# ELU of the second products on ScalarE and VectorE alone, with difference steps and buffers moved

## The chip, the cores and the metric

The kernel runs on one core of a Trainium2 chip. The metric is the time of one execution on the device, in microseconds (us), as the median of several runs. The engines are TensorE (PE; its weight loads stand apart as PEld), VectorE (DVE), ScalarE (ACT), GpSimd (POOL) and the queue of SyncE (SP), which here only issues transfers.

## What is computed

The reference is attention in which a query sees only the keys of its own cluster, and behind it a two-layer network with ELU between the layers. All is float32; the network has 3072 tokens, a width of 512 and a hidden width of 2048.

```python
scores = np.where(mask, scale * np.matmul(q, k.transpose(0, 1, 3, 2)), -1000000000.0)
attn = softmax(scores)                      # rows; mask: same cluster
x = np.matmul(attn, v)                      # (4, 8, 768, 64) -> (3072, 512)
h = x @ w_in                                # (3072, 2048)
g = np.where(h > 0.0, h, np.exp(np.minimum(h, 0.0)) - 1.0)
out = g @ w_out                             # (3072, 512)
```

## The kernel before

**Stages.** First come 32 attention blocks. Then the network follows in three pairs of 512-token groups, numbered k_ = 0 to 5. For each pair a first product computes h for 1024 tokens at once, and two second products (one for each k_) multiply ELU(h) by w_out. Both kinds of product are one level of a fast matrix product with seven multiplications in place of eight, and the second products use it on two levels.

**First products.** The one for k_ = 0 and 1 (`first_pair`) is plain float32. Those for k_ = 2, 3 and 4, 5 (`k_phase(0)` and `k_phase(1)`) multiply in a packed form: each operand of tokens is split into three parts (`x_split`, four steps: ScalarE, VectorE, ScalarE, VectorE) in a buffer `xh0` or `xh1` of 3 x 1024 columns, in turn, and the split weights are read from memory into a ring of three slots (`w_ring`, two loads for a unit, 512 KB and 256 KB). A phase has 28 units; seven operands serve four units each. `minus` steps on VectorE make the token differences. TensorE writes into four double banks; ScalarE scales one bank into another (L1378), VectorE adds results (L1341). The result is four quadrants of h: c11, c21 (used by the even k_) and c12, c22 (used by the odd k_), 8 x 512 columns each.

**ELU.** For c11 and c21 of the packed products, ELU is in the phase itself: `k_exp` (ScalarE Exp, then a POOL TENSOR_SCALAR that cuts at 1) and `k_elu` (one VectorE end, L1150). For c12 and c22 it comes later, in parts of 128 x 1024 elements:

- of the first pair, c22 in `second_product_first` through `elu_steps` (`k_exp` and `k_elu`, four parts), while c12 is done in `first_pair` with two ScalarE steps (Exp, and Relu of 1 - e, L1269 and L1270) and one VectorE end (`first_elu`, L1411);
- of the later pairs in the even second product through `elu_in_products`: three parts of c12 by Exp and Relu on ScalarE, a POOL TENSOR_SCALAR (L1488) and a DMA that POOL issues and that adds into the target (L1491); the other five parts by `k_exp` and `k_elu`.

**Second products.** `second_product_first` runs the first three units (M1, M2, M3) of k_ = 0 directly. Then `chain` runs units back to back, seven a k_ in the order M1, M2, M3, M7, M6, M5, M4. A unit has seven small products m1 to m7 of 128 x 128 tiles. m1 and m5 of the next unit are issued inside the present one, so the order on TensorE is m6, m2, next m1, m7, next m5, m3, m4. VectorE makes four differences for the next unit (`t_step`, L1588 t1, L1590 t2, L1592 t3, L1594 t4, 128 x 512), adds what ScalarE set aside (L1544, L1561), and adds results (`take`, L1620; sums L1639); ScalarE copies banks (L1500, L1504, L1537, L1558). m5 needs the next unit's t1, m6 its t2, m7 its t3, m4 its t4, and each t overwrites what the present unit's product has just read. Behind m6, m2, m7 and m4 of each unit, `note` places other work by a table: the block differences `g_step` (L1606, two halves of 128 x 1024 each), the late ELU and, in k_ = 3, splits for the next packed product. The order on each engine is the order in which the program issues.

`table_first` and `table_last` make weight sums for the second level (L930 to L937 on VectorE; L997 and accumulating DMAs L999 issued by POOL) and `weigh_step` the sums L402 to L406. Weight tables are kept in memory and read back (L1079).

**Buffers.** When the first two second products are over, the pool that holds `p_out` (4608 columns; the output rows of k_ = 0 and 1 lie in the first 2048, t of k_ = 1 behind them) and `spare` (3072 columns) is released, and a new pool takes its bytes from the low end up. A tile of the new pool waits for users of old tiles on its bytes:

```python
k_e[:] = [lowest.tile([P, 2, 512], F32, name=f"k_e{n}") for n in range(2)]
xh.append(lowest.tile([P, 3, 2, 512], F32R, name="xh1"))
w_ring.append(lowest.tile([P, 3, 512], F32R, name="ring2"))
aside_of[1] = lowest.tile([P, 1024], F32, name="aside")
k_load(2, (0, 1), nc.scalar)
k_load(2, (2,), nc.scalar)
```

So `k_e` lies on the output rows, `xh1` on the rest of p_out and 512 columns of spare, `ring2` and `aside` on spare. The two loads into `ring2` are issued by ScalarE ahead of its work for the packed product.

## Time and profile before

| | us |
|---|---|
| median of 3 runs | 880.17 (877.0 to 880.77) |
| the profiled execution | 877.92 |
| its span in the trace | 876.2 |
| TensorE busy | 844.6 |
| VectorE busy | 762.9 |
| ScalarE busy | 495.0 |
| POOL busy | 171.6 |

Times in rows are us from the span's start; a group's row ends with busy time and the mean of one instruction in ns, and the engine's idle time just before such instructions, with what ended it. In the trace k_ = 0's direct units begin at 421.2, the first packed product at 520.3, the pair k_ = 2, 3 of second products at 603.4, the second packed product at 699.6 and the pair k_ = 4, 5 at 777.2. Names in rows are those of the tiles at the program's level: xT, kq_g and w_in hold other things by then (kq_g holds c11 and c21, w_in holds c12 and c22, and xT tokens, outputs, t and streamed weights).

### The profile page before, as it was taken

The page shows a single profiled execution, that of the slowest core. Times are in us where ns is not written, and L with a number is a line of the kernel's source. Part 1 is how long each engine was busy: PE and PEld are TensorE (multiplying, and loading weights), DVE is VectorE, ACT ScalarE, POOL GpSimd, SP SyncE. Part 2 cuts the span into 40 slices and gives each one's busy share as a digit, 9 for nine tenths or more (in the row PEclk, how much of TensorE's full clock was granted, in tenths as well). Part 3 has the DMA queues.
Part 4 walks back from the last instruction along what each step waited for, and adds up shares of the span by engine and source line. Part 5 has one row for each costly group of instructions (what it writes and reads, how often), then busy time and mean ns, then how long its engine had stood idle before and what let it go on. Part 6 is the DMA issues. An engine that isn't in the chain of part 4 may idle for free.

```text
span 876.2 us, 15157 instructions
## 1 busy us (share of the span) xinstructions
PE 844.6 (96%) x5584; PEld 590.2 (67%) x5584; DVE 762.9 (87%) x987; ACT 495.0 (57%) x813; POOL 171.6 (20%) x165
## 2 busy tenths in 40 slices
PE   9999999999999999999989998999989999998897
PEld 5444444444444443444889987878989988788897
DVE  6899999999998968978988876989998869899976
ACT  6887878786888864625431226665423266655121
POOL 0023230421223532110320000104420000044200
PEclk9999999999999999999999999999999999999999
DMA  7786796788679993999199967999967799849673
GB/s 170 158 208 177 165 254 173 158 203 189 161 217 285 303 261 128 274 281 279 42 190 252 291 205 241 290 286 326 271 182 230 215 286 296 278 118 282 166 242 129
DMA packets 185441, 194.06 MB, mean 221 GB/s; under 512 B 97680, under 2 KB 131472, under 8 KB 184336
## 3 DMA queue, kind: packets, MB, share of 16 engines
q1 hardware_dynamic: 174688, 163.32, 62.1%
q0 software_dynamic: 9552, 28.32, 16.2%
q10 hardware_dynamic: 1120, 1.38, 0.6%
q8 instruction: 46, 0.75, 0.4%
q14 instruction: 35, 0.29, 0.1%
HBM read 130.06 MB, written 51.38 MB: 207 GB/s over the span
## 4 chain that ended last, share of the span: by engine, by line
PE 71%; DVE 18%; DMA 4%; issue 3%; ACT 2%; POOL 1%; DVEq 0%; SPq 0%; POOLq 0%; ACTq 0%
PE bank L1099 20%; PE double L1331 15%; PE banks L540 11%; PE banks L1280 8%; PE o_bank L596 8%; PE d_bank L596 3%; PE banks L553 3%; DVE kq_g L1606 2%; DVE xT L1588 2%; DVE xT L1594 1%; DVE xT L1592 1%; PE d_bank L616 1%; PE banks L454 1%; DVE sums_w L580 1%; DMA k_s<-spare 1%
## 5 line engine op out<-in xcount | busy, mean ns | idle before, releaser
L1331 PE MATMUL double<-xh,ring 128*128 128x512 f32 x672 | 156.1, 393 | 4.9 <-ACT kq_g L1378 3.6
L1331 PEld LDWEIGHTS double<-xh,ring 128*128 128x128 f32 x672 | 126.7, 189 | 33.6 <-ACT kq_g L1378 4.0
L576 ACT ACTIVATE p_out<-banks 128x768 f32<-128x768 f32 x150 | 118.8, 813 | 10.0 <-PE banks L540 7.5
L596 PE MATMUL o_bank<-p_out,kq_g 128*64 128x384 f32 x600 | 102.3, 490 | 0.0
L1147 POOL TENSOR_SCALAR k_e<-k_e 128x1024 f32<-128x1024 f32 x26 | 32.6, 1258 | 274.1 <-ACT k_e L1146 274.1
L1099 PE MATMUL bank<-xT 128*128 128x128 f32 x640 | 81.6, 276 | 3.5 <-DVE xT L1588 2.8
L596 PEld LDWEIGHTS o_bank<-p_out,kq_g 128*64 128x64 f32 x600 | 40.8, 137 | 59.0 <-issue 55.7
L1099 PEld LDWEIGHTS bank<-xT 128*128 128x128 f32 x640 | 76.3, 192 | 4.2 <-DVE xT L1588 3.2
L1378 ACT ACTIVATE double<-double 128x1024 f32<-128x1024 f32 x52 | 52.3, 1009 | 43.1 <-PE double L1331 27.3
L1280 PE MATMUL banks<-xT,w_in 128*128 128x512 f32 x128 | 56.2, 595 | 2.0 <-DVE kq_g L1257 1.4
L1341 DVE TENSOR_TENSOR kq_g<-double,kq_g 128x1024 f32<-128x1024 f32 x36 | 44.0, 1221 | 11.8 <-PE double L1331 7.0
L580 DVE TENSOR_TENSOR sums_w<-p_out 128x1536 f32<-128x1536 f32 x25 | 46.2, 1848 | 9.2 <-ACT p_out L576 9.2
L1099 PE MATMUL bank<-w_out,xT 128*128 128x128 f32 x288 | 38.6, 277 | 9.2 <-DVE xT L1588 9.0
L1537 ACT COPY bank<-bank 128x128 f32<-128x128 f32 x39 | 9.8, 250 | 65.6 <-PE bank L1099 65.6
L1280 PEld LDWEIGHTS banks<-xT,w_in 128*128 128x128 f32 x128 | 24.0, 190 | 33.6 <-issue 28.8
L583 DVE TENSOR_TENSOR sums_w<-sums_w,p_out 128x1536 f32<-128x1536 f32 x25 | 44.3, 1772 | 1.8
L659 POOL DMA_DIRECT2D sums_b<-xT x28 | 17.9, 661 | 139.3 <-DVE xT L633 92.3
L654 POOL TENSOR_TENSOR xT<-xT,sums_b 128x384 f32<-128x384 f32 x32 | 43.6, 1380 | 5.0 <-DMA sums_b<-xT 3.4
L1099 PEld LDWEIGHTS bank<-w_out,xT 128*128 128x128 f32 x288 | 35.0, 192 | 10.3 <-DVE xT L1588 7.4
L540 PE MATMUL banks<-x_sum,xT 64*128 64x384 f32 x192 | 38.2, 486 | 0.7 <-ACT p_out L576 0.7
L540 PE MATMUL banks<-kq_g,xT 64*128 64x384 f32 x192 | 37.6, 483 | 0.0
L540 PE MATMUL banks<-x_sum,kq_g 64*128 64x384 f32 x192 | 37.5, 482 | 0.0
(321 smaller groups left out, 1815.6 us busy)
## 6 DMA issues: line engine op xcount, KB each, us to landing
ring<-k_s SPq DMA_DIRECT2D x32, 512.0 KB, 4.7
xT<-far_s_s SPq DMA_DIRECT2D x63, 256.0 KB, 3.6
kq_g<-in_v_dram SPq DMA_DIRECT2D x32, 384.0 KB, 5.0
ring<-k_a SPq DMA_DIRECT2D x23, 512.0 KB, 5.0
xT<-far_s_q SPq DMA_DIRECT2D x38, 256.0 KB, 3.4
xT<-far_a_s SPq DMA_DIRECT2D x37, 256.0 KB, 3.6
ring<-k_s SPq DMA_DIRECT2D x32, 256.0 KB, 4.4
k_a<-w_in SPq DMA_DIRECT2D x24, 256.0 KB, 7.1
```

Of the source, the lines that this page charges most:

```text
L540: nc.tensor.matmul(s[:, e, :HS], lhsT=kT[b % 2][pr][rows, ts(kt, P)], rhs=qT[half][pr][rows], start=first, stop=not first,)
L576: nc.scalar.activation(probs(n, kt), s[:, :, :HS], Act.Exp, scale=SCALE)
L580: nc.vector.tensor_tensor(add_four, p[0], p[1], op=Alu.add)
L583: nc.vector.tensor_tensor(add_four, add_four, four(n)[2], op=Alu.add)
L596: nc.tensor.matmul(value_bank(n)[64 * e : 64 * e + 64, :HS], lhsT=v_raw[n % 2][:, e, kt], rhs=probs(n, kt)[:, e], start=(kt == 0), stop=(k ...
L654: nc.gpsimd.tensor_tensor(x_of(n), x_of(n), r, op=Alu.mult)
L1099: nc.tensor.matmul(bank[:, :P], lhsT=left[:, f], rhs=right[:, f], start=first and f == 0, stop=last and f == 3, skip_group_check=True,)
L1147: nc.gpsimd.tensor_scalar(k_e[u % 2], k_e[u % 2], 1.0, 0.0, op0=Alu.min, op1=Alu.max)
L1280: nc.tensor.matmul(bank[:, j], lhsT=w[a][:, ch, QS * u + P * j : QS * u + P * j + P], rhs=x[:, ch], start=ch == 0, stop=ch == 1,)
L1331: nc.tensor.matmul(bank[:, j], lhsT=w[:, m, QS * ch + P * j : QS * ch + P * j + P], rhs=x[:, m, ch], start=first and ch == 0 and m == part ...
L1341: nc.vector.tensor_tensor(to, x, y, op=Alu.add)
L1378: nc.scalar.activation(at(into[0], u) if n < 2 else b, a, Act.Copy, scale=K_OF)
```

## The change

- Every late ELU part takes three steps: ScalarE Exp, ScalarE Relu (scale -1, bias 1), one VectorE end (`first_elu`). `elu_steps`, `elu_in_products`, their POOL steps and accumulating DMAs go. c12 is done in four parts of two blocks as before, c22 in four parts by columns (its left half, used by b21, first).
- Their places: c22's left half of the first pair in `second_product_first` and at m4 of unit 3 of k_ = 0, its right half in unit 0 of k_ = 1; for the later pairs parts 0 to 5 (and the ScalarE steps of part 6) in the even product, the end of part 6 and part 7 in unit 0 of the odd product.
- `g_step`: the first differences of k_ = 0 move from behind unit 0 to unit 2; in the other products the eight halves run from m7 of unit 0 to m2 of unit 4, one or two a unit, instead of two in each of units 1 to 4.
- In the packed products the split of the second operand has its steps at n = 0, 2, 3, 4 instead of 0, 0, 1, 1, and `minus` of the first phase at n = 0, 1, 3, 6 instead of 0, 1, 2, 3.
- The split buffers are three tiles each. In the lower pool the order is now ring2, aside (512 columns instead of 1024), xh1, k_e: ring2 lies on the output rows, k_e on spare, and xh1 where it was.

```diff
-            plan(on_act, 4 * i, x_split, q, 0)
-            plan(on_dve, 4 * i, x_split, q, 1)
-            plan(on_act, 4 * i + 1, x_split, q, 2)
-            plan(on_dve, SECOND_PART[i], x_split, q, 3)
-        for n, x in enumerate(((t1, x12, x11), (t2, x22, t1), (x12, x22, x12), (x21, x21, t2))):
+            for what, (of, n) in enumerate(zip((on_act, on_dve, on_act, on_dve), SPLIT_AT[i])):
+                plan(of, n, x_split, q, what)
+        for n, x in zip(
+            ((0, 1, 3, 6), (0, 1, 2, 3))[part],
+            ((t1, x12, x11), (t2, x22, t1), (x12, x22, x12), (x21, x21, t2)),
+        ):
             plan(on_dve, n, minus, *x)
...
-    SECOND_PART = (1, 5, 10, 14, 17, 22)
+    SPLIT_AT = [(0, 2, 3, 4)]
+    SPLIT_AT += [(4 * n, 4 * n, 4 * n + 1, m) for n, m in ((1, 5), (2, 10), (3, 14), (4, 17), (5, 22))]
...
+    def relu_of_exp(step, x, e):
+        if step == 0:
+            nc.scalar.activation(e, x, Act.Exp)
+        elif step == 1:
+            nc.scalar.activation(e, e, Act.Relu, scale=-1.0, bias=ones[:, :1])
+        else:
+            first_elu(x, e)
+
+    def late_part(n):
+        if n < 4:
+            return of_unit(s_of[2], n)
+        n -= 4
+        return s_of[3][:, 4 * (n % 2) : 4 * (n % 2) + 4, QS * (n // 2) : QS * (n // 2) + QS]
...
-            if at in ("m2", "m7") and n == 1:
-                g_step(k_, 3, at == "m7")
-            elif at in ("m2", "m7") and 2 <= n <= 4:
-                g_step(k_, (0, 2, 1)[n - 2], at == "m7")
-            if k_ >= FIRST_IN and not k_ % 2:
-                elu_in_products(n, at)
+            for step, x in ELU_STEPS[1 if k_ == 1 else 2 + k_ % 2].get((n, at), ()):
+                late_elu(step, x, dead_e[x % 2] if k_ == 1 else k_e[x % 2])
+            if (n, at) in G_STEPS:
+                g_step(k_, *G_STEPS[n, at])
...
+    for x, n, to in (
+        (0, 0, (0, "m4")),
+        (1, 1, (2, "m4")),
+        (2, 2, (3, "m4")),
+        (3, 3, (5, "m6")),
+        (4, 4, (5, "m4")),
+        (5, 5, (6, "m7")),
+    ):
+        for step, at in enumerate(((n, "m6" if n < 5 else "m2"), (n, "m2" if n < 5 else "m7"), to)):
+            even.setdefault(at, []).append((step, x))
+    for step, at in enumerate(((6, "m6"), (6, "m2"))):
+        even.setdefault(at, []).append((step, 6))
+    odd[0, "m6"] = [(2, 6), (0, 7)]
+    odd[0, "m2"] = [(1, 7)]
+    odd[0, "m4"] = [(2, 7)]
...
+    AT_FIRST = {(0, 1): [(0, 4)], (0, 2): [(1, 4)], (1, 0): [(0, 5)], (1, 1): [(1, 5)], (2, 3): [(2, 4)]}
...
-                if n > 0 or q_ in (1, 3):
-                    next(rest_of_elu, None)
+                for x in AT_FIRST.get((n, q_), ()):
+                    late_elu(*x, k_e[x[1] % 2])
+                if n == 2 and q_ in (1, 2):
+                    g_step(0, 0, q_ - 1)
...
-                for part in range(2):
-                    g_step(0, n, part)
...
+    w_ring.append(lowest.tile([P, 3, 512], F32R, name="ring2"))
+    aside_of[1] = lowest.tile([P, 512], F32, name="aside")
+    xh.append([lowest.tile([P, 2, 512], F32R, name=f"xh1{x}") for x in "hlm"])
     k_e[:] = [lowest.tile([P, 2, 512], F32, name=f"k_e{n}") for n in range(2)]
-    xh.append(lowest.tile([P, 3, 2, 512], F32R, name="xh1"))
-    w_ring.append(lowest.tile([P, 3, 512], F32R, name="ring2"))
-    aside_of[1] = lowest.tile([P, 1024], F32, name="aside")
```

More of the change, by code (lines that the diff above doesn't have):

```diff
@@ L1132, in x_split @@
         src, to = k_operands(part)[i], xh[q % 2]
[L1133 removed]
+        h, l = (x.bitcast(F32) for x in to[:2])
         if n == 0:
[L1135 removed]
+            split_minus(to[0], src)
         elif n == 1:
[L1137 removed]
+            nc.vector.tensor_tensor(to[1], src, h, op=Alu.add)
         elif n == 2:
[L1139 removed]
+            nc.scalar.activation(to[1], l, Act.Copy, scale=-4096.0)
         else:
[L1141 to L1143 removed]
+            nc.vector.scalar_tensor_tensor(to[2], h, -1.0, l, op0=Alu.mult, op1=Alu.subtract)
     def k_exp(x, u):
@@ L1160, in ahead_of_k @@
             )
-            xh.append(upmost.tile([P, 3, 2, 512], F32R, name="xh0"))
+            xh.append([upmost.tile([P, 2, 512], F32R, name=f"xh0{x}") for x in "hlm"])
             w_ring.extend(upmost.tile([P, 3, 512], F32R, name=f"ring{x}") for x in range(2))
@@ L1257, in result @@
                 nc.vector.tensor_tensor(to, bank, of_unit(plus[i], u), op=Alu.add)
-            if i == 5:
-                late_elu.append(of_unit(c22, u))
             if i in (1, 5, 6):
@@ L1298, in first_pair, with in_columns, late_elu @@
         assert not wait
-    late_elu = []
-    def elu_steps():
-        for n in range(len(late_elu) + 2):
-            if n > 1:
-                k_elu(late_elu[n - 2], n)
-            if n < len(late_elu):
-                k_exp(late_elu[n], n)
-            yield
+    def relu_of_exp(step, x, e):
[5 more added lines that the diff above has]
+            first_elu(x, e)
+    def in_columns(x):
+        if x.shape[1] == 2:
+            return x.rearrange("p a (b n) -> p a b n", b=2)
+        return x.rearrange("p (a b) n -> p a b n", a=2)
+    def late_part(n):
[3 more added lines that the diff above has]
+        return s_of[3][:, 4 * (n % 2) : 4 * (n % 2) + 4, QS * (n // 2) : QS * (n // 2) + QS]
+    def late_elu(step, n, e):
+        x = late_part(n)
+        if n > 3:
+            x, e = in_columns(x), in_columns(e)
+        relu_of_exp(step, x, e)
     def k_phase(part):
@@ L1449, in note @@
                     table_last("a22", last, 1)
+                    late_elu(2, 5, k_e[1])
                 elif (n, at) == (5, "m6"):
@@ L1480, in main_path @@
     }
-    def elu_in_products(n, at):
-        c12, c22 = s_of[2:]
-        if n in (0, 2, 4) and at in ("m6", "m2"):
-            x, e = of_unit(c12, n // 2), k_e[0]
-            if at == "m6":
-                nc.scalar.activation(e, x, Act.Exp)
-                nc.gpsimd.tensor_scalar(e, e, 1.0, -1.0, op0=Alu.min, op1=Alu.add)
-            else:
-                nc.scalar.activation(x, x, Act.Relu)
-                nc.gpsimd.dma_start(x, e, accum_op=Alu.add)
-        of = [*(of_unit(c22, u) for u in range(4)), of_unit(c12, 3)]
-        if at == "m6" and 0 < n < 6:
-            k_elu(of[n - 1], 1)
-        elif at == "m7" and n < 5:
-            k_exp(of[n], 1)
+    G_STEPS = {
+        (0, "m7"): (3, 0),
+        (1, "m2"): (3, 1),
+        (1, "m7"): (0, 0),
+        (2, "m2"): (0, 1),
+        (2, "m7"): (1, 0),
+        (3, "m2"): (2, 0),
+        (3, "m7"): (2, 1),
+        (4, "m2"): (1, 1),
+    }
+    dead_e = [X[:, 2 * n : 2 * n + 2, :GS] for n in range(2)]
+    even, odd = {}, {}
+    for x, n, to in (
[13 more added lines that the diff above has]
+    odd[0, "m4"] = [(2, 7)]
+    after_first = {
+        (0, "m6"): [(0, 6)],
+        (0, "m2"): [(1, 6), (0, 7)],
+        (0, "m7"): [(1, 7), (2, 6)],
+        (0, "m4"): [(2, 7)],
+    }
+    ELU_STEPS = [{}, after_first, even, odd]
     def seven_first(u):
```

10 lines of the change are left out of this document (1 added, 9 removed).

## The prediction

> **What bounds the kernel now.** I read the page's head and chain, then the busy time by stages, then in the two kinds of stage where TensorE is not full the groups, the waits and the timeline.
>
> ```profile
> span 876.2 us, 15157 instructions
> ...
> PE 71%; DVE 18%; DMA 4%; issue 3%; ACT 2%; POOL 1%; DVEq 0%; SPq 0%; POOLq 0%; ACTq 0%
> ```
>
> VectorE holds 18% of the chain, and the stages show where. In the fence below the columns are stretch, its length, then busy time (and instructions) of PE, weight loads, VectorE, ScalarE and POOL, the granted clock, the DMA share and GB/s.
>
> ```profile
> 435.60:451.00 15.40, 10.38 (x85) 9.82 (x85) 12.89 (x19) 3.49 (x8) 4.37 (x5) 0.99 1.18 226
> 451.00:454.50 3.50, 3.50 (x20) 3.50 (x20) 3.50 (x7) 0.52 (x2) 0.00 (x0) 0.55 0.62 34
> ...
> 520.00:529.00 9.00, 5.41 (x26) 4.22 (x25) 1.91 (x5) 1.98 (x3) 0.00 (x0) 1.00 0.85 291
> 529.00:533.00 4.00, 4.00 (x12) 3.14 (x11) 4.00 (x4) 1.96 (x2) 0.00 (x0) 0.57 0.05 12
> ...
> 603.50:647.00 43.50, 37.76 (x332) 37.05 (x331) 41.98 (x60) 18.79 (x48) 20.41 (x11) 1.00 0.88 264
> 647.00:699.60 52.60, 51.34 (x456) 50.96 (x456) 45.19 (x94) 14.16 (x47) 0.00 (x0) 1.00 0.68 206
> ...
> 777.20:821.00 43.80, 38.01 (x334) 37.30 (x333) 42.35 (x61) 18.79 (x48) 20.49 (x11) 1.00 0.73 211
> ```
>
> Four places lose time. In 435.6 to 451 (the first second product, k_ = 0) PE works 10.38 of 15.40 us, so 5.02 are idle, and the next 3.5 us run at a clock of 0.55, which is 0.45 x 3.5 = 1.6 us more. At 520 to 529 (start of the first packed product) 3.59 us are idle, again followed by a stretch at 0.57. In 603.5 to 647 and 777.2 to 821 (the products of k_ = 2 and 4, "even" below) PE works 37.76 of 43.50 and 38.01 of 43.80: 5.74 and 5.79 idle. The same product for k_ = 3 ("odd", most of 647 to 699.6) idles 1.26 us in 52.6, with POOL at zero. So even and odd differ by POOL, and by what it does to VectorE:
>
> ```profile
> L1606 DVE TENSOR_TENSOR kq_g<-kq_g 128x1024 f32<-128x1024 f32 x8 | 11.0, 1369 | 0.0
> L1588 DVE TENSOR_TENSOR xT<-kq_g 128x512 f32<-128x512 f32 x6 | 6.2, 1040 | 0.0
> L1150 DVE SCALAR_TENSOR_TENSOR w_in<-k_e,w_in 128x1024 f32<-128x1024 f32 x5 | 6.1, 1212 | 0.0
> L1592 DVE TENSOR_TENSOR xT<-kq_g 128x512 f32<-128x512 f32 x6 | 5.9, 985 | 0.0
> L1594 DVE TENSOR_TENSOR xT<-kq_g,xT 128x512 f32<-128x512 f32 x6 | 4.7, 786 | 1.5 <-PE bank L1099 1.5
> L1590 DVE TENSOR_TENSOR xT<-kq_g,xT 128x512 f32<-128x512 f32 x6 | 4.7, 783 | 0.0
> ...
> L1606 DVE TENSOR_TENSOR w_in<-w_in 128x1024 f32<-128x1024 f32 x8 | 9.7, 1214 | 0.0
> L1588 DVE TENSOR_TENSOR xT<-w_in 128x512 f32<-128x512 f32 x7 | 4.8, 682 | 0.0
> L1590 DVE TENSOR_TENSOR xT<-w_in,xT 128x512 f32<-128x512 f32 x7 | 4.8, 679 | 0.0
> L1594 DVE TENSOR_TENSOR xT<-w_in,xT 128x512 f32<-128x512 f32 x6 | 4.1, 690 | 3.5 <-PE bank L1099 3.5
> L1592 DVE TENSOR_TENSOR xT<-w_in 128x512 f32<-128x512 f32 x6 | 4.1, 688 | 1.3 <-PE bank L1099 1.2
> ...
> L1488 POOL TENSOR_SCALAR k_e<-k_e 128x1024 f32<-128x1024 f32 x3 | 11.6, 3851 | 8.8 <-ACT k_e L1487 8.8
> ```
>
> The first block is even (604 to 648), the second odd (648 to 692), the last POOL in the even stretch; after the bar stand busy time and the mean of one. The same differences of two halves in SBUF take 1040 against 682 ns, 985 against 688, 786 against 690, 783 against 679, and the G steps (L1606) 1369 against 1214. The ELU's end (L1150) at 1212 is not stretched: it comes after POOL is done. Who waits in the even stretch:
>
> ```profile
> PE bank L1099 <- DVE xT L1588: 6.4, 4, 2.8
> ...
> PE bank L1099 <- ACT aside L1558: 0.4, 1, 0.4
> ```
>
> Four of TensorE's waits there are for t1 on VectorE (L1588), 6.4 us in all; ScalarE's copies cost it 0.4.
>
> **The change part by part.**
>
> *Even products without POOL (k_ = 2, 4).* Removed: eight TENSOR_SCALAR on POOL and three accumulating DMAs that it issues. VectorE loses the stretch: 8 x (1.369 - 1.214) = 1.24, 6 x (1.040 - 0.682) = 2.15, 6 x (0.985 - 0.688) = 1.78, 6 x (0.786 - 0.690) = 0.58, 6 x (0.783 - 0.679) = 0.62, together 6.4 us. Added: VectorE makes eight ends a pair of products where it made five; six fall in the even one, two in the odd, so even +1 x 1.21 and odd +2 x 1.21 = 2.4. Even VectorE work goes from 41.98 to 41.98 - 6.4 + 1.2 = 36.8 us, under TensorE's 37.76. The G steps start two half units earlier, which spreads them over units 0 to 4. ScalarE's price per part:
>
> ```profile
> L1270 ACT ACTIVATE sums_b<-sums_b,ones 128x1024 f32<-128x1024 f32 x12 | 13.8, 1148 | 0.4
> L1146 ACT ACTIVATE k_e<-w_in 128x1024 f32<-128x1024 f32 x5 | 5.3, 1058 | 8.3 <-DVE w_in L1150 8.3
> ```
>
> A part is Exp 1.06 and Relu 1.15 us. Before it had eight Exp and three Relu in the even stretch, now seven of each (six complete parts, and 6 begun): 18.79 + 7 x 2.21 - 11 x 1.06 = 22.6 of 43.5 us, hidden as work. As an order it is not: Exp of part n writes buffer n mod 2 and waits for the VectorE end of part n - 2, and the copies between banks stand behind it in ScalarE's queue. The tight place is unit 5, where part 5's Exp (after m2) waits for part 3's end (after m6) behind the sums of M6; then Exp runs just when the copy of the next m1 is due. I price it at one Exp, 1.1 us, and 0.7 for all other places, near the odd stretch's 1.26 idle. So an even product keeps 1.8 of 5.74 idle: -3.9, twice, **-7.8**. Ends: the whole idle time goes (-11.5), or the hole goes but each of four Exp that can be held by a buffer costs 1.1: 5.74 - 4.4 = 1.3 a product, -2.6. The accumulating DMAs that vanish were waited for by nobody; nothing.
>
> *Odd products and k_ = 1.* They get two ends (k_ = 3, 5) or two whole parts (k_ = 1, unit 0). In unit 0 VectorE has four t steps (2.7), two ends (2.4) and a G step (1.2), just 6.3 us, and TensorE takes 56 passes, 51.34 / 456 = 0.113 each, 6.3 us. Balanced, so I charge 0.2 to 0.3 each: **+0.7** in all; ends 0 and 3 x 2.4 = +7.2 if nothing hid, nearest the first because the odd window leaves VectorE 52.6 - 45.2 = 7.4 us free.
>
> *The first second product (k_ = 0).* The timeline:
>
> ```profile
> 421.20 14.45 PE L1099 MATMUL bank<-w_out,kq_g 128*128 128x128 f32 x128
> ...
> 426.08 2.29 DVE L402 TENSOR_TENSOR p_out<-w_out 128x2048 f32<-128x2048 f32 x1
> ...
> 431.33 3.12 DVE L406 TENSOR_TENSOR words_w<-w_out,p_out 128x2048 f32<-128x2048 f32 x1
> 434.38 2.35 DVE L1606 TENSOR_TENSOR kq_g<-kq_g 128x1024 f32<-128x1024 f32 x2
> ...
> 436.98 7.71 PE L1099 MATMUL bank<-sums_b,kq_g 128*128 128x128 f32 x64 [1.32 <-DVE p_out L1620]
> ...
> 443.30 2.05 DVE L1150 SCALAR_TENSOR_TENSOR w_in<-xT,w_in 128x1024 f32<-128x1024 f32 x1 [2.51 <-POOL xT L1147]
> ...
> 448.42 0.68 DVE L1588 TENSOR_TENSOR xT<-kq_g 128x512 f32<-128x512 f32 x1
> ...
> 449.15 1.05 PE L1099 MATMUL bank<-words_w,xT 128*128 128x128 f32 x7 [3.57 <-DVE xT L1588]
> ```
>
> TensorE runs 128 passes to 435.65, waits 1.32 us for a take that VectorE reaches only after two G steps (434.38, 2.35 us), and 3.57 us for t1 (448.42). VectorE is late since weight sums of 2048 elements that take 2.29 us (L402) take up to 3.12 (L406) while POOL works, since four ends of 1.21 stand between table steps, and since one of these waits 2.51 us for POOL, whose queue is held by the accumulating DMAs of the a22 table. After: the sums end some 0.8 us sooner or more, the takes follow at once (no 1.32), and ahead of t1 stand four takes and five table steps of 0.7 or less that end near 439; the G steps come later, in n = 2. TensorE gets to m5 after 64 + 8 more passes, at 435.65 + 72 x 0.113 = 443.8, so t1 is there 5 us early. TensorE then has no hole there and by these rows no half clock after it. Of 5.02 + 1.6 = 6.6 I take **-6.3**. What is late next is t4 (about 446, used near 449) and VectorE's next units. Low end: t1 early but the first take still late and a hole left that halves the clock, -3; high end -6.6. One end moves to unit 3 (after m4), 1.2 us in a unit whose VectorE work is about 6.2 of 6.3; covered, or 1.2 if not.
>
> *The moved buffers and the start of the packed product.* The lower pool is laid out anew: the third ring slot lies on the bytes where p_out's output rows were, the scratch of ELU higher up. The split buffer keeps its bytes there, in three tiles.
>
> ```profile
> 517.83 3.85 SPq L1648 DMA_DIRECT2D out_dram<-p_out  x4
> ...
> 520.04 0.84 ACTq L1122 DMA_DIRECT2D ring<-k_a  x2
> ...
> 526.64 1.06 ACT L1019 ACTIVATE xh<-xT 128x1024 fp32r<-128x1024 f32 x1 [7.99 <-DMA out_dram<-p_out]
> 527.61 1.01 ACT L1378 ACTIVATE kq_g<-double 128x1024 f32<-128x1024 f32 x1
> ...
> 528.66 11.70 PE L1331 MATMUL double<-xh,ring 128*128 128x512 f32 x43 [3.59 <-ACT kq_g L1378]
> ...
> DMA to landing us min/median/max: 2.1/2.9/6.2
> ring<-k_a ACTq DMA_DIRECT2D x1, 512.0 KB, 4.5
> ```
>
> The last two rows are times from issue to landing, of all output stores and of the first ring load (512 KB, median 4.5). Now the ring loads go out on ScalarE's queue at 520.04 without waiting for the stores; then ScalarE's first split (L1019) waits 7.99 us for the stores of p_out, although its own bytes lie past the rows that are stored: the wait is for p_out's users as a whole. After, the ring loads wait for the same stores, at the head of ScalarE's queue; behind them stand the split and the copy (L1378) for which TensorE waits. Without 768 KB of ring loads ahead of them, the stores (issued up to about 521.3) should land in 2.1 to 2.9 us, near 524, where now 5 us lie between their last issue and 526.64. Then two issues (0.84), split and copy: copy done near 527.0, where it was 528.6. But unit 2 needs the ring: 524.3 + 4.5, beside SP's own ring loads some 0.7 more, 529.5 against 528.66: **+0.9**, with the same spell at half clock. Ends: -1.6 (the ring lands by 527), and +4 (the stores still end at 526.6, the ring lands 0.4 + 4.5 and more later, or waits for SP's loads). I take the value near the quick stores because the ring loads were what ran beside the slow one. The later VectorE steps (t differences first, second split part at n = 2, 3, 4) take VectorE's long wait off its queue; the split is needed at n = 4, two units after the late one: covered, else a split's 1.06.
>
> **Sum.** -7.8 + 0.7 - 6.3 + 0.9 = -12.5 us. The profiled execution took 877.92 (span 876.2), 2.25 below the median of the runs shown (877.0 to 880.77): 865.4 from it, 867.7 from the median; I say 866.
>
> **Two rules of the skill.** The Trainium skill, "Perfetto Trace Analysis", Optimizing Scalar/DVE Operations, says that with VectorE saturated, work may be moved to Scalar or even GpSimd, and that GpSimd's only port is VectorE's second pair, so that this may not help. Its first half speaks against three more ends on VectorE and gives rival 1; the trace bears out the second half by 1040 against 682 ns. The Trainium skill, "TensorE: Matmul & The Clock Gate", What's actually happening, gives half clock after an idle window of about 3.4 us on a free-running grid; by it the holes of 3.57 and 3.59 us would seldom be caught, the trace has both caught, and if a longer hole at 525 escaped, the sum would be 1.6 lower.
>
> **Rivals.**
> 1. VectorE stays the bound of the even products: 36.8 us of work is 97% of TensorE's 37.76, and an order with late t1 still costs. Each even product then gives 1.3, the sum is -7.3: 871 to 873. For it: four waits for t1 now. Against: odd, with VectorE at 45.2 of 52.6, idles little.
> 2. The late ring: +4 in place of +0.9, sum -9.4: 869 to 871. For it: ScalarE waited 7.99 us for exactly these stores. Against: landings of 2.1 to 2.9 elsewhere.
> 3. Slower: ScalarE's queue. Each Exp held by a buffer holds the copies behind it. There are about 16 parts in the two pairs of products; the gain of 12.5 is gone if each costs TensorE 0.8 us, and at 1.2 it is 16 x 1.2 - 12.5 = 6.7 slower: 885 to 887. For it: two activations a part where the c22 parts had one. Against: 22.6 of 43.5 us busy, 0.4 us of waits now.
> 4. No change: the even products gain 1.3 each, k_ = 0 only 3, the ring costs 4, odd units 2: 878 to 881.
>
> **How the numbers follow.** Main 0.58, rivals 0.17, 0.13, 0.06 and 0.06. The range holds main, 1 and 2: from 860 (877.9 with -11.5 and -6.6) to 873. A difference of 0.5%, 4.4 us, is about what can be told from none. Faster: main, 1 and 2, 0.88; same 0.06; slower 0.06.
>
> **What would show it.** In the even windows POOL 0, L1588 and L1592 near 690 ns, PE busy 41 or more of 43.5. Around 436 to 451 no PE hole and a clock of 1.0. At the packed product's start the ring loads issued after the stores, and TensorE waiting for the ring. Wrong if waits for ScalarE's copies grow past 3 us an even product, if t1 still heads TensorE's waits, or if the ring lands past 531.

## The result, and the profile after

The changed kernel takes 865.0 us (median of 4 runs, 863.0 to 866.7) where the kernel before takes 878.8 in the same comparison (4 runs, 877.0 to 880.8): a ratio of 0.984, 95% interval 0.981 to 0.988. The forecast was 866.0 with a range of 860 to 873. The profiled execution took 865.28 us, with a span of 863.4, so 12.6 us less than the profiled one of before.

The head of the page, and of the chain of the work that ended last:

```profile
span 863.4 us, 15123 instructions
...
PE 841.2 (97%) x5584; PEld 587.9 (68%) x5584; DVE 754.9 (87%) x993; ACT 509.1 (59%) x827; POOL 123.7 (14%) x139
...
PE 79%; DVE 9%; DMA 7%; ACT 3%; issue 2%; POOL 0%; SPq 0%; DVEq 0%; ACTq 0%; POOLq 0%
```

VectorE's share of the chain has halved, from 18% to 9%; DMA's has grown from 4% to 7%. Both halves of the story are in this line. To see where the time went, the next table cuts the execution at the first matmul of each stage (columns: length in us); the last stage ends with the last matmul. In the kernel before these bounds are 421.2, 520.3, 603.35, 699.35, 777.0 and 871.5.

| stage | before | after | change | forecast |
|---|---|---|---|---|
| all ahead of k_ = 0's direct units (nothing edited there) | 421.2 | 423.2 | +2.0 | 0 |
| k_ = 0 and 1 | 99.1 | 92.8 | -6.3 | -6.05 |
| first packed product | 83.1 | 85.9 | +2.8 | +0.9 |
| pair k_ = 2, 3 | 96.0 | 90.3 | -5.7 | -3.65 |
| second packed product | 77.65 | 77.5 | -0.15 | 0 |
| pair k_ = 4, 5 | 94.5 | 89.1 | -5.4 | -3.65 |

(The forecast's 0.7 for odd products and k_ = 1 is spread over the three stages that hold them.) The sum, -12.7, is the forecast's -12.5, but three of its terms are not: the pairs gained 3.8 more than forecast, the packed product lost 1.9 more, and the stages ahead, in which no line was edited, came out 2.0 longer. In all the runs below they ended between 417.7 and 427.4. That spread is larger than most of the effects in question, so from here on I compare stages and not whole times. The stages differ in this too: the pair k_ = 2, 3 took 90.3 in all six kernels below that leave it as it is in the changed one, while the first packed product took 84.5 to 87.6 in the seven that leave its layout and its split steps alone, so its +2.8 is uncertain by a microsecond and more.

Busy time by stages of the changed kernel (stretch, length, busy time and instructions of PE, weight loads, VectorE, ScalarE, POOL, granted clock, DMA share, GB/s):

```profile
437.70:452.00 14.30, 14.30 (x130) 14.30 (x129) 13.56 (x20) 2.88 (x12) 1.86 (x2) 1.00 1.18 203
...
516.30:527.00 10.70, 4.89 (x21) 3.79 (x20) 4.99 (x5) 2.88 (x3) 0.00 (x0) 0.89 0.70 243
527.00:531.00 4.00, 4.00 (x10) 3.10 (x10) 0.00 (x0) 0.59 (x1) 0.00 (x0) 0.50 0.04 10
602.00:645.00 43.00, 41.86 (x375) 41.67 (x374) 40.17 (x71) 21.27 (x52) 0.00 (x0) 1.00 0.75 240
645.00:692.40 47.40, 46.48 (x413) 46.10 (x413) 44.16 (x87) 17.19 (x49) 0.00 (x0) 1.00 0.71 222
769.80:813.00 43.20, 42.06 (x377) 41.87 (x376) 40.37 (x72) 21.45 (x52) 0.00 (x0) 1.00 0.61 186
```

Below, a hole is a stretch in which TensorE is idle, and half clock a granted clock near 0.5. Where before PE idled 5.02 us in k_ = 0 and then ran at half clock, it is now busy 14.30 of 14.30 us at a clock of 1.00. The even products idle 1.14 us each (43.00 - 41.86, 43.20 - 42.06) where they idled 5.74 and 5.79. The start of the packed product idles 5.81 us, more than the 3.59 of before, and is followed by half clock again.

The even product's groups (busy time, mean ns of one, idle time before it) and then TensorE's waits in the pair k_ = 2, 3:

```profile
L1637 DVE TENSOR_TENSOR kq_g<-kq_g 128x1024 f32<-128x1024 f32 x8 | 9.7, 1216 | 0.0
...
L1298 ACT ACTIVATE k_e<-w_in 128x1024 f32<-128x1024 f32 x7 | 7.4, 1062 | 5.3 <-DVE w_in L1424 5.3
...
L1619 DVE TENSOR_TENSOR xT<-kq_g 128x512 f32<-128x512 f32 x6 | 4.1, 683 | 0.0
L1621 DVE TENSOR_TENSOR xT<-kq_g,xT 128x512 f32<-128x512 f32 x6 | 4.1, 680 | 0.0
```

```profile
PE bank L1099 <- ACT aside L1589: 1.1, 1, 1.1
PE bank L1099 <- DVE xT L1619: 0.7, 1, 0.7
PE bank L1099 <- DVE bank L1575: 0.2, 1, 0.2
```

With POOL silent, t1 (now L1619) takes 683 ns where it took 1040, and a G step (L1637) 1216 where it took 1369. The even product's one wait of 1.1 us for ScalarE's copy (L1589) is the place that the prediction named: at unit 5, part 5's Exp runs just when the copy of the next m1 is due. The rows of 0.7 and 0.2 lie in the odd product.

The start of the first packed product, from the timeline (start, length, then what ended the idle time), and then the times from issue to landing of the loads into the ring:

```profile
513.57 3.85 SPq L1679 DMA_DIRECT2D out_dram<-p_out  x4
...
518.13 14.12 SPq L1122 DMA_DIRECT2D ring<-k_a  x5
...
519.47 0.84 ACTq L1122 DMA_DIRECT2D ring<-k_a  x2
...
520.36 1.06 ACT L1019 ACTIVATE xh1h<-xT 128x1024 fp32r<-128x1024 f32 x1 [5.98 <-issue]
...
526.62 0.77 PE L1342 MATMUL double<-xh0h,ring 128*128 128x512 f32 x1 [5.81 <-DMA ring<-k_a]
```

```profile
ring<-k_a SPq DMA_DIRECT2D x3, 512.0 KB, 3.8
...
ring<-k_a ACTq DMA_DIRECT2D x1, 512.0 KB, 7.0
...
ring<-k_a ACTq DMA_DIRECT2D x1, 256.0 KB, 8.0
```

The stores of the output rows, the last issued by 517.4, no longer run beside 768 KB of ring loads. ScalarE's queue is released at 519.47, 2.1 us later, and the split and the copy for which TensorE had waited are early. But now TensorE waits for the ring itself, whose 512 KB land 7.0 us after their issue; I had counted on 5.2.

### The profile page after: what moved, and what is told of

It reads as the page before. It is cut to its first block, busy times and chain, and to the rows that moved or that the text cites. A ratio compares the mean times of both kernels' runs of the same rounds, so it can differ in the third digit from the quotient of the medians.

```text
span 863.4 us, 15123 instructions
## 1 busy us (share of the span) xinstructions
PE 841.2 (97%) x5584; PEld 587.9 (68%) x5584; DVE 754.9 (87%) x993; ACT 509.1 (59%) x827; POOL 123.7 (14%) x139
## 4 chain that ended last, share of the span: by engine, by line
PE 79%; DVE 9%; DMA 7%; ACT 3%; issue 2%; POOL 0%; SPq 0%; DVEq 0%; ACTq 0%; POOLq 0%
PE bank L1099 28%; PE double L1342 16%; PE banks L540 11%; PE banks L1276 8%; PE o_bank L596 8%; PE banks L553 3%; PE d_bank L596 3%; DMA k_a<-w_in 2%; DMA kq_g<-in_v_dram 1%; DMA k_a<-spare 1%; PE d_bank L616 1%; DMA sums_b<-xT 1%; DMA k_s<-spare 1%; PE banks L454 1%; DMA ring<-k_a 1%
## 5 line engine op out<-in xcount | busy, mean ns | idle before, releaser
L1145 POOL TENSOR_SCALAR k_e<-k_e 128x1024 f32<-128x1024 f32 x16 | 19.7, 1231 | 289.8 <-ACT k_e L1144 204.3
L1342 PE MATMUL double<-xh0h,ring 128*128 128x512 f32 x112 | 44.8, 400 | 5.8 <-DMA ring<-k_a 5.8
L1342 PE MATMUL double<-xh0l,ring 128*128 128x512 f32 x112 | 44.6, 398 | 0.0
L1342 PE MATMUL double<-xh1h,ring 128*128 128x512 f32 x112 | 43.7, 390 | 0.0
L1342 PE MATMUL double<-xh1l,ring 128*128 128x512 f32 x112 | 43.6, 389 | 0.0
L540 PE MATMUL banks<-kq_g 64*128 64x384 f32 x192 | 37.6, 483 | 0.4 <-ACT p_out L576 0.4
```

Source lines behind the costliest of these rows:

```text
L540: nc.tensor.matmul(s[:, e, :HS], lhsT=kT[b % 2][pr][rows, ts(kt, P)], rhs=qT[half][pr][rows], start=first, stop=not first,)
L1342: nc.tensor.matmul(bank[:, j], lhsT=w[:, m, QS * ch + P * j : QS * ch + P * j + P], rhs=x[m][:, ch], start=first and ch == 0 and m == part ...
```

## The experiments

Each kernel is the changed one with the edit shown. Where one run was made, I read its stages; where five rounds were made, the time is given too.

**The start of the packed product: four layouts and orders.** Theory: a tile that lies on bytes of p_out waits for the stores of the output rows, whatever it is; the ring is the tile for which this costs most. First, the order of before (k_e and most of xh1 on p_out's bytes, ring2 and aside on spare):

```diff
+    k_e[:] = [lowest.tile([P, 2, 512], F32, name=f"k_e{n}") for n in range(2)]
+    xh.append([lowest.tile([P, 2, 512], F32R, name=f"xh1{x}") for x in "hlm"])
     w_ring.append(lowest.tile([P, 3, 512], F32R, name="ring2"))
     aside_of[1] = lowest.tile([P, 512], F32, name="aside")
-    xh.append([lowest.tile([P, 2, 512], F32R, name=f"xh1{x}") for x in "hlm"])
-    k_e[:] = [lowest.tile([P, 2, 512], F32, name=f"k_e{n}") for n in range(2)]
```

> The changed kernel with the lower pool in the old order (ELU scratch on the output rows, split buffer in three tiles where it was, third ring slot and aside on spare); all else as changed. Theory (the third ring slot, loaded only after the stores and then beside SyncE's ring loads, makes the hole of 5.81 us): the ring loads go out before the stores are done, the hole is again the 3.6 us of the kernel before, set by ScalarE's first split, with half clock behind it; first packed product 83 us as before instead of 85.9. Rival (the stores themselves or the moved split and difference steps make the hole): it stays at 5.8.

Measured: the first packed product took 83.4 us (changed kernel 85.9, before 83.1). From its timeline at the start of this stage:

```profile
520.18 1.06 ACT L1019 ACTIVATE xh1h<-xT 128x1024 fp32r<-128x1024 f32 x1 [8.27 <-DMA out_dram<-p_out]
...
522.21 0.50 PE L1342 MATMUL double<-xh0h,ring 128*128 128x512 f32 x1 [3.83 <-ACT kq_g L1390]
```

This is the picture of before: the split waits for the stores, 8.27 us, and TensorE for the copy behind it. So the moved buffers alone cost 2.5 us against the changed kernel's profiled run, and 1.1 to 2.4 against six of the seven other kernels with its layout and split steps (84.5 to 85.75).

Second, neither the ring nor the first third of the split on p_out's bytes:

```diff
-    w_ring.append(lowest.tile([P, 3, 512], F32R, name="ring2"))
-    aside_of[1] = lowest.tile([P, 512], F32, name="aside")
-    xh.append([lowest.tile([P, 2, 512], F32R, name=f"xh1{x}") for x in "hlm"])
     k_e[:] = [lowest.tile([P, 2, 512], F32, name=f"k_e{n}") for n in range(2)]
+    lower_two = [lowest.tile([P, 2, 512], F32R, name=f"xh1{x}") for x in "lm"]
+    aside_of[1] = lowest.tile([P, 512], F32, name="aside")
+    w_ring.append(lowest.tile([P, 3, 512], F32R, name="ring2"))
+    xh.append([lowest.tile([P, 2, 512], F32R, name="xh1h"), *lower_two])
```

> The changed kernel with the lower pool ordered so that nothing needed early lies on the bytes of p_out: ELU scratch, second and third part of the split buffer and aside on p_out, ring slot and first part of the split buffer on spare. Theory: neither the ring loads nor ScalarE's first split wait for the stores, TensorE's hole falls from 5.8 to under 1 us and the half clock behind it (some 1.7 us) goes: 7 us faster, 858. Rival (the ring slot is late because the DMA queues are full anyway): the ring lands 7 us after an earlier issue, hole 2 to 3 us and half clock stays, 3 us faster, 862.

Measured: the packed product took 78.2 us, 7.7 less than in the changed kernel's profiled run and 6.3 less than in the shortest run with its layout and split steps (84.5); the kernel takes 858.5 us, 0.975 of the kernel before (0.973 to 0.978). Its timeline at the same place:

```profile
511.02 0.84 ACTq L1122 DMA_DIRECT2D ring<-k_a  x2
...
517.70 1.23 DVE L1137 TENSOR_TENSOR xh1l<-xT,xh1h 128x1024 fp32r<-128x1024 f32 x1 [0.28 <-DMA out_dram<-p_out]
...
519.20 0.47 PE L1342 MATMUL double<-xh0h,ring 128*128 128x512 f32 x1 [0.39 <-DMA ring<-k_a]
```

The ring loads are out at 511.02, before the packed product begins (511.25). What of the split still lies on p_out's bytes is needed only at n = 2, and the wait there has shrunk to 0.28 us. TensorE's hole is 0.39 us, and the half clock is gone with it (1.00 from 519.2 to 527).

Third, the disputed size: why 7.0 us and not 5.2? The ring loads stay behind the stores, but are issued by SyncE, in one queue with its own ring loads:

```diff
-    k_load(2, (0, 1), nc.scalar)
-    k_load(2, (2,), nc.scalar)
+    k_load(2, (0, 1))
+    k_load(2, (2,))
```

> The changed kernel with the two loads into ring2 issued by SyncE, behind the output stores and ahead of its own ring loads for units 3 and 4, in place of by ScalarE. Open: why the 512 KB landed 7.0 us after its issue where 5.2 was counted on. Theory: the loads that SyncE issues from 518.1 on share the DMA engines with it. Then, with SyncE's queue in order, ring2 goes first, lands about 4.5 us after it is issued, TensorE resumes 1.5 to 2.5 us sooner and the first packed product takes 83.5 to 84.5 us (changed kernel 85.9). Rival: the landing takes 7 us by itself so soon behind the stores: 85.5 to 86.5. Second rival: SyncE's loads for units 3 and 4 come late behind ring2 and open a hole at unit 3 or 4: over 86.5.

Measured: 81.3 us, 4.6 less than the changed kernel (3.2 less than the 84.5 above) and 2.2 less than the lower end expected. The timeline again:

```profile
520.42 9.39 SPq L1122 DMA_DIRECT2D ring<-k_a  x8
...
524.62 0.47 PE L1342 MATMUL double<-xh0h,ring 128*128 128x512 f32 x1 [2.79 <-DMA ring<-k_a]
```

The loads are issued at 520.42 and TensorE goes on at 524.62, 4.2 us later, where it took 7.0. So the long landing was the company of SyncE's loads for the units after, which in the changed kernel went out from 518.13, ahead of ring2. That ScalarE's queue is slow by itself is refuted by the first two layouts: there the same 512 KB go out on it ahead of SyncE's loads and land in 4.8 and 4.6 us, while behind SyncE's loads, in the changed kernel, the seven others with its layout and split steps and the next one below, they take 6.0 to 7.2. The Trainium skill, "DMA: Bandwidth & Descriptors", Queues, rings and completion order, says that a DMA engine takes turns, packet by packet, between the queues that have work for it; 7.0 us beside another queue's loads and 4.2 at the head of one queue agree with that. The hole shrank by 3.0 us; the other 1.6 go with the half clock, which did not follow this hole of 2.79 us (1.00 in the 4 us behind it). That part I had not counted on.

Fourth, the split and `minus` steps at their places of before:

```diff
-            ((0, 1, 3, 6), (0, 1, 2, 3))[part],
+            ((0, 1, 2, 3), (0, 1, 2, 3))[part],
...
-    SPLIT_AT = [(0, 2, 3, 4)]
+    SPLIT_AT = [(0, 0, 1, 1)]
```

> The changed kernel with the split's steps at n = 0, 0, 1, 1 and the minus steps at 0, 1, 2, 3, as before the change. Theory: these moves were worth nothing, since the ring load that waits for the stores ends TensorE's wait: the first packed product takes 85.4 to 86.4 us (changed kernel 85.9), all other stages within 0.3. Rival: VectorE is held at the head of its queue by the split's second step (which waits for ScalarE's first), and results of units 0 and 1 come late behind it: 1 us or more longer, with a second wait of TensorE for VectorE or a bank.

Measured: 84.8 us. That is outside what was expected (85.4 to 86.4), but no finding: of the seven kernels below that leave this place as it is in the changed kernel, six took 84.5 to 85.75 and one 87.6. I had taken one trace's 85.9 for the value; the expectation was too narrow. The moved split steps are worth nothing that can be told.

**The even products: is it POOL or the places?** First, the changed order, but in k_ = 2 to 5 POOL makes the second ELU step again (cut to 0..1) and VectorE the one end that goes with it (`last_elu`, L1148, 1.2 us as before):

```diff
-        relu_of_exp(step, x, e)
+        if not by_pool or step == 0:
+            relu_of_exp(step, x, e)
+        elif step == 1:
+            nc.gpsimd.tensor_scalar(flat, flat, 1.0, 0.0, op0=Alu.min, op1=Alu.max)
+        else:
+            last_elu(x, e)
...
-                late_elu(step, x, dead_e[x % 2] if k_ == 1 else k_e[x % 2])
+                late_elu(step, x, dead_e[x % 2] if k_ == 1 else k_e[x % 2], k_ > 1)
```

> The changed kernel; in k_ = 2 to 5 the second step of each late part (ScalarE Relu) is put on POOL as a TENSOR_SCALAR with min and max, the end adds -1 and takes the maximum; same number of VectorE ends, same places. Theory (POOL's work stretches VectorE's steps with two inputs in SBUF, and that made the even products late): POOL works 8 x 1.1 to 1.3 us a pair, VectorE's t steps go up by about that, 8 to 10 us in sum if every one of its us holds VectorE, and TensorE waits for t1 again; a pair of second products 1 to 4 us longer than the changed kernel's 90.4. Rival (the gain came from the earlier G steps and the spread ends): same 90.4 within 0.5, as ScalarE even gets freer.

Then the same with POOL's longer form, which the kernel before used for c12:

```diff
+            nc.gpsimd.tensor_scalar(flat, flat, 1.0, -1.0, op0=Alu.min, op1=Alu.add)
+        else:
+            nc.vector.tensor_tensor(x, x, e, op=Alu.max)
```

> As the run with the cut on POOL, but its TENSOR_SCALAR uses min and add (-1), the form that took 3.85 us in the kernel before, and the end is a plain maximum on VectorE. Theory: POOL works 8 x 3.9 = 31 us a pair, VectorE's differences are stretched more than before (6.4 us an even product there with three such and five short ones); a pair 4 to 9 us longer than 90.4. Rival (order, not POOL): 90.4 within 0.5.

Measured: the pairs took 92.1 and 90.9 with the short form, 91.8 and 90.6 with the long one (changed kernel 90.3 and 89.1). The groups of the even product, short form and then long form; t2 is L1626 and a G step L1642 here:

```profile
L1642 DVE TENSOR_TENSOR kq_g<-kq_g 128x1024 f32<-128x1024 f32 x8 | 11.2, 1395 | 0.0
...
L1322 POOL TENSOR_SCALAR k_e<-k_e 128x1024 f32<-128x1024 f32 x6 | 7.2, 1198 | 36.7 <-ACT k_e L1298 36.7
...
L1626 DVE TENSOR_TENSOR xT<-kq_g,xT 128x512 f32<-128x512 f32 x6 | 6.2, 1038 | 0.0
...
L1624 DVE TENSOR_TENSOR xT<-kq_g 128x512 f32<-128x512 f32 x6 | 4.1, 680 | 0.0
```

```profile
L1322 POOL TENSOR_SCALAR k_e<-k_e 128x1024 f32<-128x1024 f32 x6 | 23.1, 3843 | 23.2 <-ACT k_e L1298 23.2
L1642 DVE TENSOR_TENSOR kq_g<-kq_g 128x1024 f32<-128x1024 f32 x8 | 11.8, 1476 | 0.0
...
L1626 DVE TENSOR_TENSOR xT<-kq_g,xT 128x512 f32<-128x512 f32 x6 | 5.4, 892 | 0.0
```

What POOL stretches here is G steps and t2; t1 keeps its 680 ns. Against the 1216 and 680 ns of the changed kernel that is 8 x 0.179 + 6 x 0.358 = 3.6 us for six short POOL instructions, and 8 x 0.260 + 6 x 0.212 = 3.4 us for six that are three times as long: 0.6 us an instruction either way. I had expected the stretch to grow with POOL's time, and the long form to cost several us more; it cost nothing more. The timeline of the long form shows where the stretch falls:

```profile
610.00 3.89 POOL L1322 TENSOR_SCALAR k_e<-k_e 128x1024 f32<-128x1024 f32 x1 [5.88 <-ACT k_e L1298]
...
610.51 1.32 DVE L1626 TENSOR_TENSOR xT<-kq_g,xT 128x512 f32<-128x512 f32 x1
...
611.75 0.68 DVE L1628 TENSOR_TENSOR xT<-kq_g 128x512 f32<-128x512 f32 x1
...
612.56 1.21 DVE L1642 TENSOR_TENSOR kq_g<-kq_g 128x1024 f32<-128x1024 f32 x1
```

One difference near the start of POOL's instruction is stretched, by 0.64 us; t3 (L1628) and a G step (L1642) that start behind it, inside the same POOL instruction, take their usual 0.68 and 1.21 us. It is so for five of the six POOL instructions in both forms, with 0.64 to 0.88 us each; the sixth has no such difference near its start. The Trainium skill, "SBUF — State Buffer", SBUF: two separate sides, has the one that starts first hold the port pair that VectorE and POOL share for its whole instruction. The short form agrees: the stretched t2 and G steps there end 0.54 and 1.08 us behind POOL's end, as if they had waited for it. In the long form the measurement decides against it, since VectorE's instructions go on unstretched while POOL's is still under way. And half of the 3.6 us did not reach TensorE: the stage is 1.75 us longer.

Next, the changed kernel with the G steps at m2 and m7 of units 1 to 4, two a unit, without POOL and then with POOL's short form:

```diff
-        (0, "m7"): (3, 0),
-        (1, "m2"): (3, 1),
-        (1, "m7"): (0, 0),
-        (2, "m2"): (0, 1),
-        (2, "m7"): (1, 0),
+        (1, "m2"): (3, 0),
+        (1, "m7"): (3, 1),
+        (2, "m2"): (0, 0),
+        (2, "m7"): (0, 1),
...
-        (4, "m2"): (1, 1),
+        (4, "m2"): (1, 0),
+        (4, "m7"): (1, 1),
```

> The changed kernel with the G steps of all products behind k_ = 0 back in their old places (two in each of units 1 to 4). The runs with POOL's cut gave back 1.5 to 1.75 us a pair of second products, of 5.7 that the change gained. If the earlier G steps are the rest, a pair now takes about 94 us against 90.3. If VectorE without POOL has room enough for both orders, 90.3 to 91: four t steps, two G steps, one end and the adds are some 6.6 us in units 2 and 3 against TensorE's 6.3, a backlog under 1 us.

> Both together: old places of the G steps, and the second step of the late parts on POOL (min and max), in k_ = 2 to 5. If the two add, a pair takes 90.3 plus 1.75 plus what the late G steps cost alone. If they multiply (the stretched steps fall on the units that have two G steps each, and there every us is TensorE's), 93.5 to 96, near the 96.0 of the kernel before; then the stretch is worth more than 1.75 in the old order.

Measured: 91.0 and 89.5 without POOL (+0.7 and +0.35), 93.6 and 92.0 with it (+3.2 and +2.9). Alone POOL cost 1.75 and the late G steps 0.7; together they cost 3.2, not 2.45.

Last, the places of before for ELU and G steps in k_ = 2 to 5, with the accumulating DMAs on POOL, but with its computing done by ScalarE (which has about 12 us more work for that):

```diff
+            if at == "m6":
+                relu_of_exp(0, x, e)
+                relu_of_exp(1, x, e)
+                nc.scalar.activation(e, e, Act.Copy, scale=-1.0)
+            else:
+                nc.scalar.activation(x, x, Act.Relu)
+                nc.gpsimd.dma_start(x, e, accum_op=Alu.add)
...
+        if at == "m6" and 0 < n < 6:
+            relu_of_exp(2, of[n - 1], k_e[1])
+        elif at == "m7" and n < 5:
+            relu_of_exp(0, of[n], k_e[1])
+            relu_of_exp(1, of[n], k_e[1])
```

> The changed kernel, for k_ = 2 to 5 with the earlier places of the ELU steps and of the G steps, all eight parts in the even product, and the three accumulating DMAs issued by POOL, but with POOL's computing steps as ScalarE Relu (three parts with one more ScalarE copy for the sign). So POOL issues DMAs and computes nothing, and ScalarE has about 12 us more work than before the change. The pair of products took 96.0 and 94.5 before the change and 90.3 and 89.1 after it. Theory: POOL's computing on VectorE's reads made nearly all of the 5.6 us: 90.3 to 91.5 and 89.1 to 90.3. Rival: the places made half of it: 93 to 94 and 91.5 to 92.5. Second rival: POOL's part is small: over 95.

Measured: 92.1 and 90.6, between the two values expected. TensorE's waits in the pair k_ = 2, 3:

```profile
PE bank L1099 <- ACT aside L1614: 1.5, 3, 0.6
PE bank L1099 <- DVE xT L1644: 1.0, 1, 1.0
```

The three waits for ScalarE, 1.5 us, belong to the work added there; the 1.0 for t1 is in the odd product, as it was before. No wait for VectorE is left in the even one, though every place is the old one. So the four cells for a pair k_ = 2, 3 are: 96.0 with the old places and POOL, 92.1 with the new places and POOL, 92.1 with the old places and no POOL computing, 90.3 with neither (for k_ = 4, 5: 94.5, 90.9, 90.6 and 89.1). The cells are not quite pure: the second has, in the even product, six short POOL instructions and no accumulating DMAs where the first has eight, three of them long, and the third has ScalarE's added work. Either edit alone brings 3.9 of the 5.7 us; with the 1.5 us of waits for the added work taken off, POOL's computing alone could be worth up to 5.4, an estimate from these rows that no run shows. They are not two gains that add up: each by itself makes t1 early enough to remove most of one and the same hole.

**k_ = 0 and 1.** The ELU of c22 and the first differences in the order of before, without POOL:

```diff
-                if n == 2 and q_ in (1, 2):
-                    g_step(0, 0, q_ - 1)
...
                 keep_parts()
+                for part in range(2):
+                    g_step(0, n, part)
...
+    AT_FIRST = {
+        (0, 1): [(0, 4), (1, 4)],
+        (0, 3): [(0, 5), (1, 5)],
+        (1, 0): [(2, 4), (0, 6), (1, 6)],
+        (1, 1): [(2, 5), (0, 7), (1, 7)],
+        (1, 2): [(2, 6)],
+        (1, 3): [(2, 7)],
+    }
```

> The changed kernel with the order of the kernel before in the first second products and still no POOL: the two halves of the first G step behind unit 0, all four c22 parts in the three direct units with their ends between the table steps, none later. Theory (t1 was late by VectorE's queue: 2.3 us of G steps, three more ends of 1.13 ahead of it, and POOL's wait and stretch of about 4): from the direct units' start to the packed product 94 to 95.5 us against 92.8 changed and 99.1 before, t1 late by 1 to 2.5 us, no half clock. Rival (the order alone made the holes): 97 to 99, half clock back. Rival (POOL alone): 92.8.

And the changed order with POOL's short form for the four late parts of k_ = 0 and 1 (the first POOL edit above, asked for here by these calls):

```diff
-                    late_elu(2, 5, k_e[1])
+                    late_elu(2, 5, k_e[1], True)
...
-                late_elu(step, x, dead_e[x % 2] if k_ == 1 else k_e[x % 2])
+                late_elu(step, x, dead_e[x % 2] if k_ == 1 else k_e[x % 2], k_ == 1)
...
-                    late_elu(*x, k_e[x[1] % 2])
+                    late_elu(*x, k_e[x[1] % 2], True)
```

> The changed kernel with its order everywhere, but the second ELU step of the four late parts of k_ = 0 and 1 on POOL again (cut to 0..1) and the one VectorE end that goes with it. With the order of before and POOL the stage of k_ = 0 and 1 took 99.1 us; with the order of before and no POOL 93.75; with the new order and no POOL 92.8 to 93.5. Theory: what cost was VectorE waiting in its queue for a POOL held by accumulating DMAs, together with an order that put the G steps ahead; the new order has slack for a late end: 94 to 95.5. Rival: POOL alone carries all of it: 98 to 99. Second rival: POOL costs nothing once the G steps are moved: 93 to 93.7.

Measured: 93.75 with the old order and no POOL, a little under the 94 to 95.5 expected; the kernels with neither took 92.8 to 93.5, so the old order costs hardly anything by itself here. But 99.2 with the new order and POOL, as long as before, which was the rival to my theory. The time is lost elsewhere than before, though. The busy time in the stretch of k_ = 0 shown above, first with the old order and no POOL, then with the new order and POOL, and of this last kernel at the start of k_ = 1's results:

```profile
438.90:453.20 14.30, 14.05 (x120) 13.55 (x120) 14.30 (x23) 6.70 (x14) 1.86 (x2) 1.00 1.23 203
...
434.50:448.80 14.30, 14.30 (x130) 14.30 (x130) 14.13 (x21) 2.88 (x11) 7.08 (x3) 1.00 1.11 274
...
487.00:491.20 4.20, 1.62 (x14) 1.27 (x12) 4.20 (x10) 0.43 (x2) 0.00 (x0) 1.00 1.06 396
491.20:495.00 3.80, 3.80 (x19) 3.80 (x20) 3.78 (x6) 0.46 (x2) 0.00 (x0) 0.55 0.56 170
```

In k_ = 0 TensorE idles 0.25 us with the old order and no POOL, and not at all with the new order and POOL: there the new order alone hides POOL. The idle time and the half clock come some 45 us later. The timeline (its last two lines are TensorE's), and then VectorE's longest wait in the stage, say why:

```profile
439.66 5.70 POOL L1322 TENSOR_SCALAR xT<-xT 128x1024 f32<-128x1024 f32 x1
...
445.31 0.63 POOL L1759 DMA_DIRECT2D ok_far<-ok  x1
...
456.56 0.56 POOL L1760 DMA_DIRECT2D cT<-ok_far  x1 [10.62 <-DMA ok_far<-ok]
...
457.12 1.38 POOL L999 DMA_DIRECT2D sums_b<-w_out  x1
...
476.51 0.86 SPq L1684 DMA_DIRECT2D out_dram<-p_out  x2
...
488.08 1.13 PE L1099 MATMUL bank<-words_w,p_out 128*128 128x128 f32 x8 [0.62 <-issue]
...
491.16 1.91 PE L1099 MATMUL bank<-words_w,p_out 128*128 128x128 f32 x8 [1.96 <-DVE p_out L1624]
```

```profile
DVE p_out L1656 <- DMA out_dram<-p_out: 5.8, 1, 5.8
```

One POOL instruction takes 5.70 us beside a VectorE that is busy 14.13 of 14.30. POOL's queue holds behind it a small store that must come back before the accumulating DMAs of a weight table go out. In the changed kernel the store was issued 19.1 us and the DMAs 32.5 us into the stage; here 25.3 and 37.1. SyncE's queue stores that table ahead of the output rows of k_ = 0, which go out 56.5 us into the stage instead of 50.8. VectorE, which puts k_ = 1's results on the same bytes, then waits 5.8 us for them to land, and TensorE for VectorE. Each step is in the traces; that the first causes the last is read from the order of the queues and not shown, since no run holds this queue without computing on POOL. In the kernel before the rows left equally late (56.9), but TensorE had by then lost its time in k_ = 0.

**The best version.** The second layout above, and part 5's Exp one step later in unit 5, out of the way of the copy for which TensorE waited 1.1 us:

```diff
-        for step, at in enumerate(((n, "m6" if n < 5 else "m2"), (n, "m2" if n < 5 else "m7"), to)):
+        for step, at in enumerate(((n, "m6" if n < 5 else "m7"), (n, "m2" if n < 5 else "m4"), to)):
```

> The layout that keeps ring slot and first split part clear of the output rows, and in unit 5 of the even products part 5's Exp one step later (after m7) and its Relu after m4. In the changed kernel TensorE waits 1.1 us there for a ScalarE copy (L1589) that stands behind this Exp, which waits for part 3's end. Theory: that wait goes, each pair 1.0 us shorter (89.3 against 90.3), 2 us faster than with the layout alone. Rival: Exp or Relu now blocks another copy or the end of part 5 comes late: no change.

Measured: 853.1 us, 0.971 of the kernel before (0.968 to 0.974). The pairs took 89.1 and 87.9, 1.2 less each, and the packed product 78.9. The even product of k_ = 2 has no idle time left in its first 44 us:

```profile
592.15:636.15 44.00, 44.00 (x394) 43.86 (x393) 41.77 (x76) 23.38 (x55) 0.00 (x0) 1.00 0.76 249
```

## Why the prediction was right, and where its steps were not

**What bounded the kernel.** Right: four places, of which three gained, and the fourth stayed a hole. One reading was careless: the waits of 6.4 us for t1 were those of the pair; 5.4 in three waits are the even product's and 1.0 the odd one's. A second one: the ELU's end was taken to be unstretched because it comes after POOL is done, but one at 637.96 lies wholly inside a POOL instruction of 4.10 us and takes 1.21 us all the same, as the instructions behind the first stretched one did above.

**Even products (-7.8 forecast).** The unstretched VectorE and the 1.1 us for one Exp came as worked out. The step that failed is the 0.7 us "for all other places": there was nothing in them, and the odd products did not lose the 0.2 to 0.3 charged to each pair but gained 0.35 (TensorE's idle 1.26 before, 0.92 after). Of the first pair's 5.7 us that is 4.6 and 0.35; the rest stands in PE's busy time, in part since a product is listed at 1.13 to 1.16 us behind a wait and at 1.06 else. The two pairs brought 11.1 us where 7.3 net were forecast. The cause was only half told, too: I put the gain down to the stretch, and the four cells show that the new places alone, with POOL, bring 3.9 of the 5.7 us. Rival 1 (VectorE stays the bound) is refuted by 1.14 us of idle time, none of it for VectorE, with VectorE busy 40.2 of 43.0; so is rival 3 by one ScalarE wait of 1.1.

**First second product (-6.3).** Right in size and place: t1 is there at 439.2, 16.0 us into the stage (forecast 17.8), and TensorE is full. Why is less simple than the prediction had it. Either the order or the absence of POOL removes the hole in k_ = 0, and what POOL costs besides is, as argued above, the delay of its own queue, of which the prediction said nothing: it saw POOL's computing held by the DMAs, and not the DMAs held by the computing.

**The moved buffers (+0.9).** The sign, the mechanism and the quick stores were right (stores landed in 2.2 us, the ring went out at 519.5, TensorE waited for the ring). That the ring loads were what ran beside the slow stores holds in every kernel: the stores landed in 2.2 us where ring2 goes out behind them and in 3.7 to 3.9 where it goes out beside them. The mis-sized term is the landing: 4.5 + 0.7 forecast, 7.0 measured (6.0 to 7.2 in the other kernels), since ring2 goes out behind SyncE's loads and shares the engines with them. The 0.7 was an allowance without a row behind it. Rival 2's price of +4 is nearer than mine to the +2.8 of the profiled run, if for another reason than late stores; five of the seven other kernels with this layout and these split steps lie at +1.4 to +1.95, nearer to mine, the other two at +2.7 and +4.5.

**The sum.** 866.0 against 865.0 is in part luck: the pairs' 3.8 us too little were made up by 1.9 of the ring and 2.0 of stages that were not edited.

## What to carry to other kernels

When two edits each remove the same wait, the gain of both is less than the sum of the two (5.7 against 3.9 and 3.9 here); only the four cells tell, and a forecast that credits one of them can be right in size and wrong in cause. Before a buffer is put on bytes that are just being stored, ask which of the tiles is needed last, and give it those bytes: here this choice was worth 6.3 to 7.7 us, more than the change made in a pair (5.7). And a load that is needed first belongs at the head of the queue that carries the others, not beside it on another queue.
